# Attention on 64-query blocks: scores on quarters of the array, 13 transposes a pair of heads, and a split P V

## The chip, the cores and the metric

The kernel runs on one core of a Trainium2 chip. The metric is device time in microseconds (us) of one execution. The core has TensorE (PE; its weight loads are listed as PEld), VectorE (DVE), ScalarE (ACT), GpSimd (POOL) and SyncE (SP), whose queue issues all DMAs here.

## The reference

```
def _attn_ref(q, k, v):                     # 4 batches, 8 heads, 576 tokens, 64 channels
    scores = scale * np.matmul(q, k.transpose(0, 1, 3, 2))
    rel = pos[:, None] - pos[None, :]
    bias = slopes[:, None, None] * (-np.abs(rel))[None, :, :]
    mask = (rel >= 0) & (rel < 128)
    scores = np.where(mask, scores + bias[None], -1000000000.0)
    attn = np.exp(scores - max); attn = attn / (sum + 1e-09)
    return np.matmul(attn, v)
def _moe_ref(x, w1, w2, w3, w_out):   return ((x @ w1) * (x @ w2) @ w3) @ w_out     # 2304 x 512, ff 1024
def _moe2_ref(x, w_in, w_out):        h = np.maximum(x @ w_in, 0.0); return h * h @ w_out   # ff 2048
reference = _moe2_ref(_moe_ref(attention output laid out as 2304 x 512))
```

A query sees itself and the 127 keys before it. So 64 consecutive queries need at most 191 keys, and 128 consecutive queries at most 255.

## The kernel before, in words

The kernel is one program of small tasks. A planner (class `Plan`) is given each task's engine or engines, an assumed cost, the tasks that it depends on and the buffers that it holds; it lists the tasks in one order, and every engine executes its instructions in that order. A task with several possible engines (a copy, a normalisation, a conversion) gets the one that the planner picks. When costs, buffers or dependencies change, the whole order before the end of attention changes with them.

Attention works on pairs of heads: 32 heads are 16 pairs, head 2m on partitions 0 to 63 of the `qk` tile and head 2m+1 on 64 to 127. For each pair:
- `t_load_qk`, `t_load_v`: DMAs of q and k (transposed on the host) and of v into one of two fixed `v` tiles.
- `p_qk` (L451): the scores. A head is cut into four tiles of 128 queries with 128, 256, 256 and 256 keys and a last one with 192 keys, whose 64 queries stand on partitions 64 to 127. Each matmul has 64 rows (the channels) by 128 columns of the array, and the two heads alternate, so two matmuls lie on the two halves of the array. The task comes in three groups (`g` 0 to 2) into PSUM tiles `s`, of which there are four.
- `l_min` (L418, DVE): adds the bias tile `bm`, scales, and gives the row's minimum, into `e` (the last tile of a head into `p4`, named `p` in the profile). Five instructions a head.
- `l_exp` (L426, ACT): exponential with the row's sum. `l_sum` (L433, L434), then `l_norm` (L241 on DVE, L243 on ACT, L239 on POOL) divides by the sum. Five of each a head.
- `p_tr` (L467): 128 x 128 transposes of the probabilities on TensorE, nine a head in groups of four and five, into the one PSUM tile `t`; `l_pt` copies each group to `pt` (L199 on ACT).
- `p_pv` (L483): P V with v as the stationary operand, 128 rows by 64 columns of the array, the two heads on the two halves of the columns. Two groups a pair, six matmuls each, into the one PSUM tile `a`.
- `t_xh`, `t_xl`, `t_xs`: for batch 0 the result is split into a rounded part and a rest (`x`), for batches 1 to 3 it is copied to `xs` and stored to `x_scr`.

Between these tasks the planner sets those of the feed-forward part that can begin: conversions of packed weights (`raw`, L317, L326, L332, L202), w3 times w_out (`p_w34`, L589: 64 matmuls of 512 columns), and from 143 us on the first products of batch 0 (`p_ab`, L194 to L196, on `x` and `wu`). The last P V of the sixteenth pair ends at 210 us; from then on TensorE executes the rest of the two feed-forward nets.

At the start GpSimd makes the identity `ident` and the bias tile (`bm`, L220 to L228); four matmuls of `ident` and `bm` (`p_warm`, L515) stand ahead of the first scores in TensorE's order.

Of the kernel before, what the change touches and what calls it, by code (L numbers as in the profile page):

```python
# [15 lines left out]
RANK = dict(w34=4, h0=-20, w12=35.93, w12s=7.96, w12l=7.68, mg=500, mgs=4, yl=8, yn=0, hs=12)  # L16
# [7 lines left out]
NE = 3  # L24
# [7 lines left out]
class Plan:  # L32
# [27 lines left out]
    def run(self):  # L60
# [15 lines left out]
        shape = lambda n: {"qk": 1, "pv": 2}.get(n[:2], 0)  # L76
# [75 lines left out]
def fused_kernel(  # L152
# [48 lines left out]
    def sub(eng, o, a, b):  # L201
# [16 lines left out]
    bm = at.tile([128, H, 2 * WIN], F32, name="bm")  # L218
    b0 = bm[:, 0]
    nc.gpsimd.iota(  # L220
        b0, pattern=[[4, 2 * WIN]], base=-4 * WIN, channel_multiplier=-4,
        allow_small_or_imprecise_dtypes=True,
    )
    nc.gpsimd.affine_select(
        out=b0, in_=b0, pattern=[[-1, 2 * WIN]], compare_op=ALU.is_ge,
        fill=-1.0e30, base=WIN, channel_multiplier=1,
    )
    nc.gpsimd.affine_select(  # L228
        out=b0, in_=b0, pattern=[[1, 2 * WIN]], compare_op=ALU.is_gt,
        fill=-1.0e30, base=0, channel_multiplier=-1,  # L230
    )
    for h in range(1, H):
        nc.vector.tensor_scalar(out=bm[:, h], in0=b0, scalar1=0.5 ** h, scalar2=None, op0=ALU.mult)
# [38 lines left out]
    def w_dma(kb, n=1):  # L272
# [4 lines left out]
            u=11, u34=4, wo=4, qk=2, v=2, e=NE, p4=3, s=4, t=1, pt=NE, a=1, g=2, asb=2, gf=2, gt=8, ye=2,  # L277
            al=2, be=2, ga=2, d1=2, d2=2, d4=2, gq=8, xs=1, xm=1, xt1=1, xt2=1, yA=14, yB=6, s0=1, t2a=1, t2b=1, v6=6, st=2, xa=2, xb=2, xc=2, D1=2, D2=2, D4=2, D3=1, fo=4, fq=5, ww=4,
# [89 lines left out]
    QA = 384  # L368
    vt = [at.tile([128, 2, 5, D], F32, tag=f"v{i}", name=f"v{i}") for i in range(2)]
    for t in vt:  # L370
        nc.gpsimd.memset(t[64:128, :, 4, :], 0.0)
    p4 = [at.tile([128, 256], F32, tag=f"p4{i}", name=f"p4{i}") for i in range(3)]
    for t in p4:
        nc.gpsimd.memset(t, 0.0)
    stat = [at.tile([128, 3, 5], F32, tag=f"st{i}", name=f"st{i}") for i in range(4)]
    for t in stat:
        nc.gpsimd.memset(t, 1.0)
# [21 lines left out]
    def rows(i):  # L399
        return slice(64, 128) if i == 4 else slice(0, 128)  # L400

    def part_of(n, i):
        if i == 4:
            return p4[n % 3][64:128, 0:192]
        return HD[n]["e"][:, i, 128 if i == 0 else 0:256]

    def l_min(n, i):
        d = HD[n]
        bmh = bm[:, n % H]
        if i == 0:  # L410
# [12 lines left out]
    def l_exp(n, i):
        e = part_of(n, i)
        st = stat[n % 4][rows(i)]
        nc.scalar.activation(  # L426
            out=e, in_=e, func=ACTF.Exp, bias=st[:, 0, i:i + 1], scale=-1.0,
            accum_out=st[:, 1, i:i + 1],
        )

    def l_sum(n):
        st = stat[n % 4]
        nc.vector.tensor_scalar(out=st[:, 2], in0=st[:, 1], scalar1=1.0e-9, scalar2=None, op0=ALU.add)  # L433
        nc.vector.reciprocal(out=st[:, 2], in_=st[:, 2])  # L434

    def l_norm(n, i, e):
        x = part_of(n, i)
        scaled(e, x, x, stat[n % 4][rows(i), 2, i:i + 1])

    def p_qk(m, g):  # L440
# [962 lines left out]
```

## Time and profile before

| what | value |
|---|---|
| three runs | 845.72, 847.19, 847.26 us; median 847.19 |
| the profiled execution | 845.38 us, its span 843.4 us |
| granted TensorE clock | 0.999 |
| PE busy | 823.2 us (98%), 5830 matmul records |
| DVE busy | 629.7 us (75%) |
| ACT busy | 494.3 us (59%) |
| POOL busy | 61.1 us (7%) |
| DMA | 137.06 MB, mean 163 GB/s |

The span runs from the first to the last instruction; 1.98 us of the execution lie around it. TensorE's busy time is a union of records that overlap each other, so 98% does not say that no time is lost on it. An fp32 matmul leaves two records (two passes), a transpose or a matmul of the rounded type (`fp32r`) one.

### The profile page before, as it was taken

To read this page: it belongs to the slowest core of one execution; us is meant where nothing else is said; L and a number is where in the kernel's file an instruction comes from. 1 tells how busy PE (TensorE), PEld (TensorE's weight loads), DVE (VectorE), ACT (ScalarE), POOL (GpSimd) and SP (SyncE) were. 2 spreads that over 40 slices of the span, in tenths; PEclk is the share of its full clock that TensorE was granted. 3 is DMA by queue.
4 is the path that set the end of the run, shared out by engine and by line. 5 is a ranking of instruction groups with operands and counts; after the bars stand their busy time and mean duration, and the time that the engine had idled before them with its cause. 6 is when DMAs were issued, how large, how long until landed. Compare 5 with 4: busy or idle time off the path is not lost.

```text
span 843.4 us, 15493 instructions
## 1 busy us (share of the span) xinstructions
PE 823.2 (98%) x5830; PEld 752.8 (89%) x5830; DVE 629.7 (75%) x1354; ACT 494.3 (59%) x1026; POOL 61.1 (7%) x75
## 2 busy tenths in 40 slices
PE   7999999999999999999999999999999899999998
PEld 5555555879999989999999999999999799999998
DVE  7999897987689797497488574632599898767662
ACT  6997788986232361252225375744697776666531
POOL 1000010000000210030022031000112010000000
PEclk9999999999999999999999999999999999999999
DMA  9899789686423444112132364523796655444300
GB/s 277 263 305 312 247 262 271 189 286 239 126 75 121 143 154 145 49 39 65 61 107 97 132 188 150 184 102 108 235 294 205 186 157 150 138 140 133 98 33 32
DMA packets 92346, 137.06 MB, mean 163 GB/s; under 512 B 8304, under 2 KB 70256, under 8 KB 90224
## 3 DMA queue, kind: packets, MB, share of 16 engines
q1 hardware_dynamic: 92272, 136.08, 50.9%
q8 instruction: 46, 0.75, 0.4%
q14 instruction: 28, 0.23, 0.1%
HBM read 94.24 MB, written 41.81 MB: 161 GB/s over the span
## 4 chain that ended last, share of the span: by engine, by line
PE 76%; DVE 16%; ACT 4%; issue 2%; DMA 1%; POOL 0%; SPq 0%; ACTq 0%; DVEq 0%; POOLq 0%
PE xa L1061 8%; PE xa L1063 8%; PE xa L1062 8%; PE g L194 6%; PE g L195 6%; PE g L196 6%; PE xb L1061 4%; PE xb L1063 4%; PE xb L1062 4%; DVE e L418 3%; PE al L1010 3%; PE al L1012 2%; PE al L1011 2%; PE xc L1062 2%; PE xc L1061 2%
## 5 line engine op out<-in xcount | busy, mean ns | idle before, releaser
L1122 DVE TENSOR_TENSOR D<-xb,D 128x384 f32<-128x384 f32 (+1 forms) x66 | 34.0, 518 | 58.5 <-PE xb L1063 29.7
L195 PE MATMUL g<-gt,wu 128*128 128x288 f32 x256 | 75.7, 296 | 0.0
L194 PE MATMUL g<-gt,wu 128*128 128x288 f32 x256 | 75.7, 296 | 0.0
L196 PE MATMUL g<-gt,wu 128*128 128x288 f32 x256 | 75.4, 295 | 0.0
L426 ACT ACTIVATE e<-e,st 128x256 f32<-128x256 f32 (+1 forms) x128 | 60.5, 475 | 17.9 <-DVE st L418 17.5
L199 ACT ACTIVATE D<-xa 128x384 f32<-128x384 f32 (+1 forms) x102 | 46.3, 455 | 39.2 <-PE xa L1063 36.5
L589 PE MATMUL g<-raw 128*128 128x512 f32 x128 | 62.6, 604 | 0.3 <-DVE raw L332 0.3
L1010 PE MATMUL al<-x,wc 128*128 128x288 f32 x192 | 57.4, 299 | 2.0 <-ACT d L199 1.4
L202 DVE TENSOR_TENSOR ww<-fq,ww 128x1024 fp32r<-128x1024 f32 x34 | 41.6, 1223 | 23.1 <-ACT ww L199 22.7
L199 ACT ACTIVATE ww<-fq 128x1024 fp32r<-128x1024 f32 x35 | 37.0, 1058 | 34.7 <-PE xa L1063 19.7
L1012 PE MATMUL al<-x,wc 128*128 128x288 f32 x192 | 56.7, 295 | 0.0
L1011 PE MATMUL al<-x,wc 128*128 128x288 f32 x192 | 56.5, 294 | 0.0
L1152 ACT ACTIVATE D<-D 128x384 f32<-128x384 f32 x72 | 37.1, 523 | 25.5 <-DVE D L1122 25.4
L199 ACT ACTIVATE ye<-g 128x288 f32<-128x288 f32 x32 | 13.1, 410 | 66.0 <-PE g L196 61.9
L798 DVE TENSOR_TENSOR st<-st 128x256 f32<-128x256 f32 (+1 forms) x105 | 41.7, 428 | 11.1 <-DMA st<-m_scrc 6.1
L199 ACT ACTIVATE d<-al 128x288 f32<-128x288 f32 x72 | 29.2, 410 | 33.9 <-PE al L1012 26.1
L418 DVE CUSTOM_DVE_ANT_0 e<-s,bm 128x256 f32<-128x256 f32 (+1 forms) x128 | 43.3, 387 | 7.6 <-PE t L467 4.3
L195 PEld LDWEIGHTS g<-gt,wu 128*128 128x128 f32 x256 | 48.3, 189 | 0.0
L196 PEld LDWEIGHTS g<-gt,wu 128*128 128x128 f32 x256 | 48.2, 188 | 0.0
L194 PEld LDWEIGHTS g<-gt,wu 128*128 128x128 f32 x256 | 48.1, 188 | 0.1
L451 PE MATMUL s<-qk 64*128 64x256 f32 (+2 forms) x320 | 42.6, 369 | 2.5 <-DVE st L418 1.3
L483 PEld LDWEIGHTS a<-pt,v 128*64 128x64 f32 x384 | 23.6, 136 | 19.2 <-issue 5.9
(271 smaller groups left out, 2829.8 us busy)
## 6 DMA issues: line engine op xcount, KB each, us to landing
s_scr<-D SPq DMA_DIRECT2D x96, 192.0 KB, 2.0
u<-in_w2io_dram SPq DMA_DIRECT2D x22, 512.0 KB, 6.5
fo<-s_scr SPq DMA_DIRECT2D x20, 512.0 KB, 4.9
qk<-in_qk_dram SPq DMA_DIRECT2D x32, 288.0 KB, 5.6
st<-m_scrc SPq DMA_DIRECT2D x18, 512.0 KB, 3.7
raw<-in_w3t_dram SPq DMA_DIRECT2D x8, 1024.0 KB, 9.3
raw<-in_w_dram SPq DMA_DIRECT2D x8, 1024.0 KB, 6.9
fq<-s_scr SPq DMA_DIRECT2D x16, 512.0 KB, 5.0
```

The costliest lines, as they stand in the source:

```text
L194: nc.tensor.matmul(o, wh, xh, start=start, stop=False)
L195: nc.tensor.matmul(o, wh, xl, start=False, stop=False)
L196: nc.tensor.matmul(o, wl, xh, start=False, stop=stop)
L199: nc.scalar.activation(out=o, in_=i, func=ACTF.Copy)
L418: nc.vector.tensor_tensor_reduce(out=part_of(n, i), in0=ps, in1=bmi, op0=ALU.add, op1=ALU.min, scale=-0.125, scalar=3.0e38, accum_out=stat ...
L589: nc.tensor.matmul(gw[fi], wl, wr, start=c == 0, stop=c == 7)
L1010: nc.tensor.matmul(o, wh, xh, start=start and c == 0, stop=False, skip_group_check=True)
L1011: nc.tensor.matmul(o, wh, xl, start=False, stop=False, skip_group_check=True)
L1012: nc.tensor.matmul(o, wl, xh, start=False, stop=c == 1, skip_group_check=True)
L1061: nc.tensor.matmul(o, wh, xh, start=start, stop=False, skip_group_check=True)
L1062: nc.tensor.matmul(o, wh, xl, start=False, stop=False, skip_group_check=True)
L1063: nc.tensor.matmul(o, wl, xh, start=False, stop=stop, skip_group_check=True)
```

## The change

The same attention, cut otherwise. Each 64 queries get their own 192 keys; two such blocks stand above each other in a 128-row tile. A score tile is therefore 128 or 192 columns wide and never 256, and the bias comes in two new tiles, `bw` and `bz`, which GpSimd makes in five pieces (`toeplitz`). The score matmuls use 64 rows by 64 columns of the array; a tile takes four of 128 columns (the first one) or six of 192, 128 and 64. The last 64 queries of the two heads share one tile (`x` = 8), so a pair has nine exponentials and nine normalisations where it had ten of each; the minima stay ten. The probabilities of a pair stand in one tile `e` of 25 units of 64 columns; 13 transposes (in groups of 4, 4, 4 and 1) turn two units each, so that the two 64-row halves of a transposed tile can belong to different blocks of keys. P V is split: `p_pv` has 14 matmuls with 128 rows, 192 or 64 columns wide, and `p_pvl` has 14 with 64 rows by 64 columns of the array and 64 wide, which add into the same PSUM tiles; `t_load_v` loads parts of v a second time for them, to the other half of the partitions. The result leaves in pieces of 256, 64 and 256 columns instead of 384 and 192, and `xs` becomes a part of `pt`. Buffers: `e` and `pt` two of a pair each (before: three of a head), `s` three (four), `a` two (one). The first half of batch 0's products now waits for both pieces of `x`. Two weights of the planner (`w34`, `hs`) change.

```diff
-RANK = dict(w34=4, h0=-20, w12=35.93, w12s=7.96, w12l=7.68, mg=500, mgs=4, yl=8, yn=0, hs=12)
+RANK = dict(w34=3, h0=-20, w12=35.93, w12s=7.96, w12l=7.68, mg=500, mgs=4, yl=8, yn=0, hs=10)
-NE = 3
+NE = 2
+NPS = 3
...
-    ps_s = psb.enter_context(tc.tile_pool(name="ps_s", bufs=4, space=PSUM))
+    ps_s = psb.enter_context(tc.tile_pool(name="ps_s", bufs=NPS, space=PSUM))
     ps_t = psb.enter_context(tc.tile_pool(name="ps_t", bufs=1, space=PSUM))
-    ps_v = psb.enter_context(tc.tile_pool(name="ps_v", bufs=1, space=PSUM))
+    ps_v = psb.enter_context(tc.tile_pool(name="ps_v", bufs=5 - NPS, space=PSUM))
...
+    toeplitz(bz[:, 0], 0, True, False)
+    toeplitz(bw[0:64, 0, 64:256], 128, True, True)
+    toeplitz(bw[64:128, 0, 0:192], 128, True, True)
+    toeplitz(bw[64:128, 0, 192:256], 128, False, True)
+    toeplitz(bw[0:64, 0, 0:64], 0, True, False)
     for h in range(1, H):
-        nc.vector.tensor_scalar(out=bm[:, h], in0=b0, scalar1=0.5 ** h, scalar2=None, op0=ALU.mult)
+        nc.vector.tensor_scalar(out=bw[:, h], in0=bw[:, 0], scalar1=0.5 ** h, scalar2=None, op0=ALU.mult)
+        nc.scalar.activation(out=bz[:, h], in_=bz[:, 0], func=ACTF.Copy, scale=0.5 ** h)
...
-        nc.sync.dma_start(out=v[0:64, :, 4, :], in_=v_rest[b, 2 * p:2 * p + 2].rearrange("h p d -> p h d"))
+        nc.sync.dma_start(
+            out=v[64:128, :, 4:6, :].rearrange("p h c d -> p h (c d)"),
+            in_=v_main[b, 2 * p:2 * p + 2, 0:64, 2 * D:4 * D].rearrange("h p c -> p h c"),
+        )
+        nc.sync.dma_start(out=v[0:64, :, 4, :], in_=v_main[b, 2 * p:2 * p + 2, 64:128, 0:D].rearrange("h p d -> p h d"))
+        nc.sync.dma_start(out=v[0:64, :, 5, :], in_=v_rest[b, 2 * p:2 * p + 2].rearrange("h p d -> p h d"))
...
+        for i in ((0, 1, 2), (3, 4))[g]:
+            o = (0, 128, 320, 0, 192)[i]
+            if i == 0:
+                todo += [(r, x, 0, x, 0, 128) for x in range(2) for r in range(2)]
+            elif i == 4:
+                todo += [(r, r, o, 8, 6, 192) for r in range(2)]
+            else:
+                late = [i + 4 * r in LEFT_FIRST for r in range(2)]
+                todo += [(r, late[r], o, 2 * i + late[r], 2 * i - 2 + late[r], 192) for r in range(2)]
+                todo += [(r, 1 - late[r], o + 64 * late[r], 2 * i + 1 - late[r], 2 * i - 2 * late[r], 128) for r in range(2)]
+                todo += [(r, 1 - late[r], o + 128 - 128 * late[r], 2 * i + 1 - late[r], 2 * i - 1 + late[r], 64) for r in range(2)]
...
     PV = (
-        ((0, 0, 0, 256), (1, 128, 256, 256), (2, 256, 512, 128)),
-        ((3, 0, 768, 192), (2, 0, 640, 128), (4, 128, 960, 64)),
+        lambda r: ((0, 0, 512 * r, 192), (1, 192, 512 * r + 192, 64), (3, 256, 1152 + 192 * r, 64)),
+        lambda r: ((1, 0, 512 * r + 256, 64), (2, 64, 512 * r + 320, 64), (2, 128, 1024 + 192 * r, 64), (3, 192, 1088 + 192 * r, 64)),
     )
...
+    def p_pvl(m):
+        pt, v = PR[m]["pt"], vt[m % 2]
+        up, down = slice(0, 64), slice(64, 128)
+        todo = (
+            (0, up, 1, 128, lambda r: 512 * r + 384), (1, down, 5, 128, lambda r: 512 * r + 384),
+            (0, up, 4, 192, lambda r: 512 * r + 448), (1, down, 2, 192, lambda r: 512 * r + 448),
+            (1, down, 4, 0, lambda r: 1408 * r), (0, up, 5, 256, lambda r: 1408 + 64 * r),
+            (1, down, 1, 64, lambda r: 64 + 1408 * r),
+        )
...
-    XC = ((0, QA), (QA, S))
+    XC = (((0, 0, 256), (256, 512, 64)), ((0, 256, 256),))
...
-    W = (128, 256, 256, 256, 192)
+    W = (128, 192, 192, 192, 192)
...
-                [f"xl{g_}_{4 * b + k}" for g_ in range(hf + 1) for k in range(K1)] + [f"chw12{fi}", f"clw12{fi}", "gp"] + after
+                [f"xl{g_}_{4 * b + k}" for g_ in range(2) for k in range(K1)] + [f"chw12{fi}", f"clw12{fi}", "gp"] + after
```

How the instructions move is shown at three places; a row is an instruction with its line, what it writes and reads, the shape written, and how many alike follow each other. First TensorE in the early part, before: the first two groups of one pair's scores (L451), the transposes of a head (L467) and the first group of P V (L483), with w3 times w_out (L589) between them.

```order
L451 MATMUL s<-qk 128x128 x2
L451 MATMUL s<-qk 128x256 x6
L467 MATMUL t<-ident,e 128x128 x4
L589 MATMUL g<-raw 128x512 x2
L467 MATMUL t<-ident,p_139 128x128 x2
L467 MATMUL t<-ident,e 128x128 x3
L589 MATMUL g<-raw 128x512 x2
L483 MATMUL a<-pt,v_135 64x256 x4
L483 MATMUL a<-pt,v_135 64x128 x2
```

Now, on TensorE, the first group of a pair's scores (L467) and what stands behind it (L659 is w3 times w_out, L503 the transposes):

```order
L467 MATMUL s<-qk 64x128 x4
L467 MATMUL s<-qk 64x192 x2
L467 MATMUL s<-qk 64x128 x2
L467 MATMUL s<-qk 64x64 x2
L467 MATMUL s<-qk 64x192 x2
L467 MATMUL s<-qk 64x128 x2
L467 MATMUL s<-qk 64x64 x2
L659 MATMUL g<-raw 128x512
L503 MATMUL t<-ident,e 128x128 x4
```

Where two matmuls of 256 columns made one score tile of each head, six narrower ones on 64 columns of the array now do; the first group of scores holds 16 instructions in place of four. Second, on TensorE, P V of a pair now, with the last transpose ahead of it (L527 is `p_pv`, L543 is `p_pvl`):

```order
L503 MATMUL t<-ident,e 128x128
L527 MATMUL a<-pt,v_162 64x192 x2
L527 MATMUL a<-pt,v_162 64x64 x12
L543 MATMUL a<-pt,v_162 64x64 x8
L543 MATMUL a<-pl,v_162 64x64
L543 MATMUL a<-pt,v_162 64x64 x3
L543 MATMUL a<-pl,v_162 64x64
L543 MATMUL a<-pt,v_162 64x64
L659 MATMUL g<-raw 128x512 x3
```

The two groups of P V stand together and the quarter matmuls directly behind them, where before other work stood between the two groups. Third, GpSimd's first instructions, before:

```order
masks.py:197 MEMSET ident 128x128
L220 ISA
L220 IOTA bm 128x256
masks.py:199 AFFINE_SELECT ident<-ident 128x128
L224 AFFINE_SELECT bm<-bm 128x256
L371 MEMSET v_134 64x2x64
L228 AFFINE_SELECT bm<-bm 128x256
```

and now (`bz` and `bw` are the bias tiles):

```order
masks.py:197 MEMSET ident 128x128
L224 ISA
L224 IOTA bz 128x128
masks.py:199 AFFINE_SELECT ident<-ident 128x128
L229 AFFINE_SELECT bz<-bz 128x128
L224 IOTA bw 64x192 x2
L229 AFFINE_SELECT bw<-bw 64x192 x2
L234 AFFINE_SELECT bw<-bw 64x192 x2
L224 IOTA bw 64x64 x2
L234 AFFINE_SELECT bw<-bw 64x64
L229 AFFINE_SELECT bw<-bw 64x64
```

The last instruction on which the first matmul of TensorE waits (it reads `bw`) is the fourteenth there, counted without the row `ISA`, where it was the sixth.

## Rows read from the trace of the kernel before

**Rows 1.** Busy time by stretch: stretch, length, PE, PEld, DVE, ACT, POOL, clock, DMA share, GB/s.

```profile
8.00:66.00 58.00, 53.91 (x333) 33.11 (x331) 55.21 (x194) 54.97 (x148) 0.60 (x1) 1.00 0.92 299
66.00:104.00 38.00, 37.85 (x201) 20.59 (x203) 34.10 (x97) 27.59 (x71) 0.43 (x1) 1.00 0.84 278
104.00:172.00 68.00, 66.36 (x474) 45.45 (x471) 60.38 (x221) 60.75 (x181) 3.05 (x7) 1.00 0.82 238
172.00:212.00 40.00, 39.66 (x333) 33.70 (x332) 32.27 (x115) 30.34 (x84) 0.83 (x2) 1.00 0.79 270
212.00:843.00 631.00, 620.15 (x4475) 616.17 (x4474) 444.96 (x722) 319.14 (x544) 52.67 (x46) 1.00 0.40 128
```

**Rows 2.** The chain of waits by line, in 8 to 66, 104 to 172, 172 to 212 us.

```profile
by line: DVE e L418 20.3%; DVE raw L332 16.3%; DVE e L241 13.8%; DVE raw L326 7.7%; DVE p L418 6.1%; ACT raw L317 5.2%; DVE x L202 4.6%; issue 4.4%; DVE p L241 3.3%; DVE st L434 3.1%; ACT pt L199 2.7%; ACT p L426 1.9%; DVE st L433 1.9%; ACT
...
by line: DVE e L418 15.6%; DVE e L241 9.6%; DVE wu L202 7.9%; ACT e L426 7.4%; issue 5.5%; DVE raw L332 5.4%; DVE u L332 5.2%; ACT pt L199 3.9%; DVE p L418 3.8%; DVE p L241 3.3%; DVE raw L326 3.0%; DVE st L434 2.9%; ACT p L426 2.4%; PE s L4
...
by line: PE a L483 20.6%; PE t L467 19.3%; PE g L194 16.4%; PE g L195 14.9%; PE g L196 14.6%; PE s L451 11.9%; DVE u L332 3.1%; DVE e L418 1.6%; ACT pt L199 0.4%; issue 0.4%; DVE st L418 0.1%; ACTq L199 0.1%
```

**Rows 3.** TensorE's records on tile `a` (P V) by stretch: length, busy, records.

```profile
8.00:66.00 58.00, 8.72 (x96) 1.00 0.92 299
66.00:104.00 38.00, 4.70 (x52) 1.00 0.84 278
104.00:172.00 68.00, 12.75 (x144) 1.00 0.82 238
172.00:212.00 40.00, 8.72 (x96) 1.00 0.79 270
```

**Rows 4.** Pieces of the chain, 84 to 196 us: start, us until the next piece, records.

```profile
84.20 1.72 PE g L589 x4
...
87.15 1.72 PE s L451 x16
...
179.95 0.53 PE s L451 x4
180.47 0.81 PE a L483 x12
181.28 0.59 PE t L467 x4
...
195.55 1.23 PE a L483 x12
```

**Rows 5.** Groups by line and shape, 0 to 212 us: count, busy us, mean ns.

```profile
L426 ACT ACTIVATE e<-e,st 128x256 f32<-128x256 f32 x96 | 47.8, 500 | 1.0 <-DVE st L418 0.9
L199 ACT ACTIVATE pt<-t 128x512 f32<-128x512 f32 x64 | 37.7, 589 | 4.2 <-PE t L467 2.9 <-PE a L483 0.6
L418 DVE CUSTOM_DVE_ANT_0 e<-s,bm 128x256 f32<-128x256 f32 x96 | 36.5, 420 | 0.2
...
L241 DVE TENSOR_SCALAR e<-e,st 128x256 f32<-128x256 f32 x78 | 23.8, 356 | 0.0
...
L426 ACT ACTIVATE p<-p,st 64x192 f32<-64x192 f32 x32 | 14.4, 450 | 2.3 <-DVE st L418 1.7
...
L418 DVE CUSTOM_DVE_ANT_0 p<-s,bm 64x192 f32<-64x192 f32 x32 | 11.4, 361 | 1.3 <-PE s L451 0.3
...
L241 DVE TENSOR_SCALAR p<-p,st 64x192 f32<-64x192 f32 x23 | 7.4, 320 | 0.5
```

**Rows 6.** The chain at the start, same columns as rows 4.

```profile
0.73 0.12 POOL ident masks.py:197
...
2.25 0.41 POOL bm L228
2.70 3.70 PE t L515 x8
```

**Rows 7.** TensorE's timeline: two P V matmuls, 64 wide, alone: start, us, shape, records.

```profile
188.83 0.28 PE L483 MATMUL a<-pt,v 128*64 128x64 f32 x4
```

**Rows 8.** DMA of 0 to 215 us.

```profile
DMA packets 21237, 56.33 MB, mean 262 GB/s; under 512 B 4112, under 2 KB 8288, under 8 KB 19168
```

More of the change, by code (lines that the diff above doesn't have):

```diff
@@ L365, in add_weights @@
         add("cl" + k, rank, w_tt(1024), lambda e: conv_lo(key, e), ["ch" + k], [], ["raw" + k])
[L368 to L377, printed above, removed]
+    vt = [at.tile([128, 2, 6, D], F32, tag=f"v{i}", name=f"v{i}") for i in range(2)]
+    stat = [at.tile([128, 3, 9], F32, tag=f"st{i}", name=f"st{i}") for i in range(2)]
     HD = [dict() for _ in range(B * H)]
@@ L426, in l_exp @@
         nc.scalar.activation(
-            out=e, in_=e, func=ACTF.Exp, bias=st[:, 0, i:i + 1], scale=-1.0,
-            accum_out=st[:, 1, i:i + 1],
+            out=e, in_=e, func=ACTF.Exp, bias=st[:, 0, x:x + 1], scale=-1.0,
+            accum_out=st[:, 1, x:x + 1],
         )
     def l_sum(n):
[L432 to L438, printed above, removed]
+        m, r = divmod(n, 2)
@@ new lines, in p_qk, with p_tr @@
+        for a in todo:
+            mm(*a)
+    def p_tr(m, g):
+        e = PR[m]["e"]
+        t = PR[m]["t", g] = ps_t.tile([128, 512], F32, tag="t", name="t")
+        if g < 2:
+            todo = [(t[:, 128 * i:128 * i + 128], u) for i, u in enumerate(((0, 2, 8, 4), (11, 13, 23, 15))[g])]
+        elif g == 2:
+            todo = [
+                (t[:, 0:128], 6), (t[:, 128:512].rearrange("p (a c) -> p a c", c=192)[:, :, 0:64], 19),
+                (t[:, 192:320], 17), (t[:, 384:512], 21),
+            ]
+        else:
+            todo = [(t[:, 0:128], 9)]
+        for o, u in todo:
+            nc.tensor.transpose(o, e[:, u:u + 2, :].rearrange("p u c -> p (u c)"), ident)
@@ L480, in p_pv @@
         o = PR[m][g] = ps_v.tile([128, 512], F32, tag="a", name="a")
-        for x, (kb, c, src, w) in enumerate(PV[g]):
+        pt = PR[m]["pt"]
+        for x in range(len(PV[g](0))):
+            for r in range(2):
+                kb, c, src, w = PV[g](r)[x]
+                nc.tensor.matmul(
+                    o[64 * r:64 * r + 64, c:c + w], vt[m % 2][:, r, kb, :], pt[:, src:src + w],
+                    start=x == 0, stop=False, skip_group_check=True,
+                )
+    def p_pvl(m):
[6 more added lines that the diff above has]
+            (1, down, 1, 64, lambda r: 64 + 1408 * r),
+        )
+        for x, (g, rows, kb, c, src) in enumerate(todo):
@@ L514, in p_warm @@
         for _ in range(k):
-            nc.tensor.matmul(t[:, 0:w], ident, bm[:, 0, 0:w], start=True, stop=True)
+            nc.tensor.matmul(t[:, 0:w], ident, bw[:, 0, 0:w], start=True, stop=True)
     plan.filler = p_warm
@@ new lines, in add_pair @@
+                    [f"qk{i // 3}_{m}"] + ([f"mi{i - 1}_{n}"] if i else []) + ([f"mi0_{n - 1}"] if j and not i else []),
+                    [f"e_{m}"] if i == 0 and j == 0 else [], [f"s{i // 3}_{n}"],
+                )
+                if i < 4:
+                    add(f"ex{4 * j + i}_{m}", rj + 2.1, {"a": 0.29 + W[i] * 0.00086}, lambda e, i=i, j=j: l_exp(m, 4 * j + i), [f"mi{i}_{n}"])
+        add(f"ex8_{m}", r + 4.1, {"a": 0.29 + 192 * 0.00086}, lambda e: l_exp(m, 8), [f"mi4_{n}" for n in heads])
@@ L575, in add_pair @@
+        if b < NS:
+            hold(xn, f"x_{p}", 4 * NF1)
+        for g in range(2):
+            cost = {}
+            for _, _, w in XC[g]:
+                for k, v in w_copy(w, True).items():
+                    cost[k] = cost.get(k, 0) + v
+            add(f"xh{g}_{m}", r + 9, cost, lambda e, g=g: t_xh(m, g, e),
+                [f"pvl_{m}"] + ([f"xh0_{m}"] if g else []), [xn] if b < NS and not g else [], [f"{'ab'[g]}{m}"])
             if b < NS:
-                add(f"xl{g}_{m}", r + 9, w_tt(w, "d"), lambda e, g=g: t_xl(m, g), [f"xh{g}_{m}"], [], [f"{'ab'[g]}{m}"])
+                add(f"xl{g}_{m}", r + 9, {"d": sum(w_tt(w, "d")["d"] for _, _, w in XC[g])}, lambda e, g=g: t_xl(m, g),
+                    [f"xh{g}_{m}"], [], [f"{'ab'[g]}{m}"])
@@ L577, in add_pair @@
         if b >= NS:
[L578 removed]
+            add(f"sx{m}", r + 9, {"dma": w_dma(295)}, lambda e: t_xs(m), [f"xh{g}_{m}" for g in range(2)], [], [f"pt_{m}"])
     gw = {}
```

212 lines of the change are left out of this document (105 added, 107 removed).

## Prediction
> **What bounds the kernel now.** I read the stretches first. From 212 us to the end TensorE is busy 620.15 of 631 us, while VectorE and ScalarE are far from full [rows 1]. The change touches nothing there, so whatever moves the end moves the end of the attention part, and what it gives is what TensorE gets to do sooner before 212 us. Before that, three engines are near their limit at once, and the chain of waits says which one ends last. From 8 to 66 us it is mostly VectorE: the minima (L418), the normalisations (L241) and the conversions of weights (L332, L326), and VectorE is busy 55.21 of 58 us [rows 1, 2]. From 66 to 104 us TensorE is busy 37.85 of 38 us [rows 1]. From 104 to 172 us the chain is again mostly VectorE, with pieces of ScalarE (L426, L199); from 172 us it is TensorE: P V 20.6%, transposes 19.3%, scores 11.9%, products of batch 0 most of the rest [rows 2].
>
> A pair leaves 24 records on tile `a`, so by [rows 3] 96/24 = 4.0 pairs lie in 8 to 66, 52/24 = 2.2 in 66 to 104, 144/24 = 6.0 in 104 to 172 and 4.0 in 172 to 212. I price the change per pair: by TensorE in the 6.2 pairs of the second and fourth stretch, by VectorE and ScalarE in the 10.0 of the others.
>
> **TensorE, a pair before.** Two matmuls of 512 columns on the whole array took 1.72 us: 1.68 ns a column [rows 4]. The 16 records of scores are eight matmuls of together 2 x 128 + 6 x 256 = 1792 columns, which one after the other would be 3.01 us; the piece is 1.72 us long [rows 4]. So the two halves of the array work at the same time: 896 columns are 1.51 us, and 0.21 us is the group's own overhead. The last group, 192 columns deep, gives 0.32 + 0.21 = 0.53, the P V group of 0.81 us 384 columns deep and 0.16 over, and that of 1.23 us 640 deep and 0.16 over [rows 4]. Four transposes behind another kind of matmul are 0.59 us; a fifth adds 128 columns of one pass, 0.11. A pair is 1.72 + 0.53 + 1.23 + 0.81 + 2 x (0.59 + 0.70) = 6.87 us.
>
> **TensorE, a pair after.** The depth of the scores is 128 + 4 x 192 = 896 columns if the four quarters of the array work at once: 1.51 us, plus 0.21 for each of two groups, 1.93. P V on full rows is 320 + 256 = 576 deep, in one block by the order rows: 0.97 + 0.16 = 1.13. The 14 quarter matmuls are four rounds of 64 columns: 0.43 + 0.16 = 0.59. The transposes are 3 x 0.59 and a single one of 0.11 + 0.16: 2.04. Sum 5.69, or 1.18 us less a pair.
>
> No row shows four quarters at work. The nearest rows are halves by rows and halves by columns, both two at a time [rows 4]. If quarters too ran only two at a time, the scores' 24 matmuls of 3200 columns would be 1600 deep, 2.69 + 0.42 = 3.11 us, and the quarter P V 448 deep, 0.75 + 0.16 = 0.91: a pair 7.19 us, 0.32 more than before. I take four at a time, because neither the split by rows nor that by columns costs anything beyond the columns in these rows. The Trainium skill, TensorEngine Tiling (Array Packing), Key Properties, says that different tiles can load weights and multiply in parallel, and lists four independent tiles of 64 x 64; the trace agrees for two, and no run here shows four.
>
> **VectorE and ScalarE, a pair.** Six of the ten minima go from 256 to 192 columns: 0.420 to 0.361 us by mean duration, 0.35 us together; by busy time (36.5/96 = 0.380 against 11.4/32 = 0.356) only 0.14 [rows 5]. Of the normalisations VectorE has 78/16 = 4.9 wide ones a pair, 0.356 to 0.320, 0.18 us (nothing by busy time), and of two last tiles one goes, 23/32 of it on VectorE: 0.23. That is 0.37 to 0.76 us a pair; the result's third piece takes a few hundredths back in four pairs. On ScalarE six exponentials go from 0.500 to 0.450 and one of 0.450 goes: 0.75. The copies out of the transposes were 4 x 0.589 and become 3 x 0.589 and one of 128 columns, which I put at 0.3 (it is under the 0.450 of 192 columns): 0.29 less. One more copy of the result a pair costs about 0.3. Together 0.74. I take 0.65 us a pair, near VectorE's upper end because most of these instructions stand in rows behind each other's waits: 10.0 x 0.65 = 6.5 us.
>
> **The start.** TensorE's first matmul waits for the bias tile: GpSimd gets from 0.73 to 2.66 us with six instructions, 0.32 each; the matmuls behind it (3.70 us) and the scores follow at once [rows 6]. Now it is the fourteenth instruction. Eight more are 2.6 us at that rate, 1.0 at the shortest piece (0.12), 3.3 at the longest (0.41); the new pieces are narrower, so I take 2.2, all of it on the path, since every engine waits for the first scores.
>
> **What costs nothing, and its cover.** v is loaded with 96 KB more a pair, 1.5 MB in all, beside 56.33 MB at 262 GB/s [rows 8]: 5.9 us of transfers, spread over 16 pairs and issued two pairs ahead. The cover is thinnest in 8 to 66 us, where the engines of the DMA are busy 0.92 of the time [rows 1]; with no cover, four pairs there cost 1.5 us. Three score tiles instead of four make the second group of scores wait for three minima of the first; behind it on TensorE stand transposes and w3 times w_out, and up to 3 x 0.361 = 1.1 us a pair would be lost. Before, six tiles a pair went through four buffers, now four through three, so I count nothing. The products of batch 0 wait for one piece of `x` more, but the four pairs that make `x` are over at 66 us [rows 3] and the products begin at 143 us. Bringing `xs` into `pt` holds that buffer until its store has landed; two pairs lie between.
>
> **The sum.** 6.2 x 1.18 = 7.3, plus 6.5, minus 2.2: 11.6 us. From the profiled execution (845.4, that is its span of 843.4 and 2.0 around it) this gives 833.8, from the median of 847.2 it gives 835.6. I forecast 835 us.
>
> **The rivals.**
> - *TensorE is the bound throughout* (0.20). In 104 to 172 us it is busy 66.36 of 68 us and in 8 to 66 us 53.91 of 58 [rows 1]; if its order, not VectorE, holds the others up, all 16.2 pairs give 1.18: 19.1 - 2.2 = 16.9 us, 830, and down to 823. Against it: the chain names VectorE there.
> - *The stretches of VectorE give nothing* (0.12), because a wait for a score tile or for a pair's buffer takes the place of the shorter instructions: 7.3 - 2.2 = 5.1 us, 842.
> - *Nothing measurable* (0.04), about 847.
> - *Quarters work two at a time* (0.10), the case on the other side. TensorE loses 0.32 in 6.2 pairs, 2.0 us; in the other ten its 3.2 us more fill what it had free, and the shorter instructions of VectorE wait for it. With the start 4.2 us, 851, at most 855. It decides from the point where a pair's work on TensorE is not shorter than 6.87 us.
> - *Narrow matmuls cost a fixed time* (0.04). A pair now has 52 matmuls, 104 records, instead of 44. Two 64-wide ones alone took 0.28 us for four records [rows 7]; put wholly down to the records it is 0.07 each, and 60 more, two at a time, are 2.1 us a pair, 0.9 net: 16 x 0.9 + 2.2 = 17 us, 864. Against it: 64 columns, two at a time, are 0.11 of the 0.28, and 0.16 over is what any group shows. The Trainium skill, TensorEngine Tiling (Array Packing), Instruction Overhead, speaks for this rival: about 60 cycles a matmul, and no tiling factor from a dimension that is already small. By it the 30 more matmuls, 60 passes of 25 ns, would be an estimated 1.5 us a pair if nothing overlapped.
>
> **How the numbers follow.** Forecast 0.50 (830 to 841), the others as given. A measurement of this kernel tells about 0.2%, 1.7 us, from no change. Faster than that: 0.50 + 0.20 + 0.12 = 0.82; same 0.04; slower 0.10 + 0.04 = 0.14. The range of 824 to 848 holds the forecast, nearly all of the first rival, the second and the third: 0.84. The forecast alone, with the bounds of VectorE (0.37 to 0.76) and of the start (1.0 to 3.3), is 830 to 841.
>
> **What would show it.** Right: the granted clock at 1.00; a pair's 24 score matmuls in about 1.9 us where they are not held up; the last P V near 200 us with the same pieces of feed-forward ahead of it, or later with more of them; minima of 192 columns near 0.36 us; the first scores at about 8.6 us. Wrong: quarter matmuls that start in twos with their full depth between; a gap on TensorE ahead of the second score group that a minimum ends; transfers of v that end a wait; or a span after the last P V that is longer than before.

## The result and the profile after

The changed kernel takes 839.17 us (median of five runs, 835.16 to 839.85), the kernel before 847.19 us in the same runs (845.63 to 848.39). The ratio is 0.990, with a 95% interval of 0.9873 to 0.9927: 8 us faster, where 12 were forecast. The profiled execution of the change took 835.16 us (span 833.4), 10.2 us less than that of before.

The time is one that the forecast allowed; the way to it is not. The stretches of [rows 1], now in the changed kernel, in the same columns:

```profile
8.00:66.00 58.00, 54.23 (x608) 34.47 (x608) 51.05 (x194) 45.94 (x138) 2.90 (x4) 1.00 0.96 298
66.00:104.00 38.00, 38.00 (x427) 22.25 (x426) 31.06 (x115) 27.85 (x86) 0.82 (x2) 1.00 0.90 276
104.00:172.00 68.00, 67.42 (x905) 53.40 (x904) 63.35 (x248) 56.55 (x184) 3.57 (x4) 1.00 0.90 270
172.00:212.00 40.00, 31.54 (x373) 28.67 (x372) 20.08 (x68) 18.57 (x56) 0.00 (x0) 0.91 0.61 188
212.00:833.00 621.00, 610.50 (x4404) 606.72 (x4402) 443.10 (x721) 317.61 (x541) 52.22 (x46) 1.00 0.43 135
```

Up to 172 us TensorE is as full as before or fuller, and it gets more done: the first products of batch 0 begin at 125.6 us (143 before). But from 172 to 212 us it is busy only 31.54 of 40 us (39.66 before). VectorE and ScalarE are idle half of that time as well, so none of the three bounds the stretch.

The chain of waits of the changed kernel from 172 us on (start, us until the next piece, what) names what does:

```profile
172.72 0.33 SPq L843
...
173.10 5.92 DMA u<-in_w2io_dram
...
179.13 1.10 ACT u L330
180.23 0.99 ACT u L335
181.22 0.16 ACT pl L200
...
194.23 7.10 DMA m_scri<-u
...
201.43 0.70 DVE wc L260
```

These are not the attention's transfers. Eight tiles of packed w2 weights are loaded (`m_load`, L843), converted on ScalarE and VectorE (L330, L335, L339, L345) and stored again (`m_store`, L849), to be fetched after 400 us. I call this a round trip. The planner sets the conversions into the same queues as the attention's copies, and there they wait for their loads: at 179.13 ScalarE has just got its load, and only behind the conversion comes the copy `pl` (L200) for which P V waits. The waits for a DMA of 120 to 212 us (who waited for what: us in total, times, longest), first the four that matter in the changed kernel, then all of those before:

```profile
ACT u L330 <- DMA u<-in_w2io_dram: 13.7, 5, 5.0
DVE wc L260 <- DMA m_scri<-u: 11.0, 2, 8.1
DVE u L339 <- DMA u<-in_w2io_dram: 3.9, 2, 2.6
DVE u L345 <- DMA m_scri<-u: 2.3, 1, 2.3
```

```profile
DVE u L326 <- DMA u<-in_w2io_dram: 1.3, 1, 1.3
DVE st L798 <- DMA st<-m_scrc: 0.9, 1, 0.9
ACT u L317 <- DMA u<-in_w2io_dram: 0.2, 1, 0.2
PEld a L483 <- DMA m_scri<-u: 0.2, 1, 0.2
```

The same eight round trips were there before, but when VectorE and ScalarE came to a conversion, its load had nearly always landed: 1.5 us of waits for these loads, now 17.6. One link lies behind this. The tiles `u` and the weights of batch 1, `wc`, take their buffers from the same eleven slots, and the slot of a stored tile comes free only when its store has landed. The loads in SyncE's queue (L843; L773 before) waited for that four times in 120 to 212 us, before only once, and `wc` waited for it on VectorE, 11.0 us in the list. First the changed kernel, then the one before:

```profile
SPq L843 <- DMA m_scri<-u: 21.3, 4, 6.2
```

```profile
SPq L773 <- DMA m_scri<-u: 4.3, 1, 4.3
```

So these loads started late, and the engines reached their conversions early; no run separates what each of the two made of the 17.6 us. (The changed kernel has one longer wait for a DMA, of GpSimd for v, 16.4 us; GpSimd has little to do there, 3.57 of 68 us.)

A pair's work on TensorE, in pieces of the chain from 108 us (to be read against [rows 4]):

```profile
108.41 0.81 PE s L467 x12
...
109.48 1.17 PE a L527 x28
110.66 0.62 PE a L543 x28
...
116.65 1.04 PE s L467 x25
```

The two groups of scores take 1.04 and 0.81 us, 1.85 together (1.93 forecast), P V 1.17 and 0.62 (1.13 and 0.59). Four quarters do work at once: two at a time, the scores would take 3.11 us. The shorter instructions of VectorE and ScalarE, by line and shape (against [rows 5]), are as expected too:

```profile
L443 ACT ACTIVATE e<-e,st 128x192 f32<-128x192 f32 x112 | 50.1, 450 | 2.4 <-DVE st L435 2.1
...
L435 DVE CUSTOM_DVE_ANT_0 e<-s,bw 128x192 f32<-128x192 f32 x96 | 31.6, 351 | 4.5 <-PE s L467 4.5
L467 PE MATMUL s<-qk 64*64 64x192 f32 x256 | 30.8, 330 | 0.5 <-DVE st L435 0.5
```

And the start is 2.3 us later (against [rows 6]; the scores came at 6.40 there):

```profile
4.66 0.24 POOL bw L229
...
4.95 3.78 PE t L569 x8
8.73 1.29 PE s L467 x17
```

### The profile page after: what moved, and what is told of

Same layout as the page of the kernel before. It is cut to its first block, busy times and chain, and to the rows that moved or that the text cites. A ratio compares the mean times of both kernels' runs of the same rounds, so it can differ in the third digit from the quotient of the medians.

```text
span 833.4 us, 17233 instructions
## 1 busy us (share of the span) xinstructions
PE 804.7 (97%) x6716; PEld 748.0 (90%) x6716; DVE 610.1 (73%) x1349; ACT 469.3 (56%) x1011; POOL 63.3 (8%) x74
## 4 chain that ended last, share of the span: by engine, by line
PE 80%; DMA 8%; DVE 6%; ACT 3%; issue 1%; SPq 1%; POOL 0%; POOLq 0%; ACTq 0%; DVEq 0%
PE xa L1131 8%; PE xa L1133 8%; PE xa L1132 8%; PE g L659 6%; PE g L195 5%; PE g L196 5%; PE g L197 5%; PE xb L1133 4%; PE xb L1131 4%; PE xb L1132 4%; DMA m_scri<-u 3%; PE al L1080 3%; PE al L1082 3%; PE al L1081 3%; PE s L467 2%; DMA u<-in_w2io_dram 2%
## 5 line engine op out<-in xcount | busy, mean ns | idle before, releaser
L195 PE MATMUL g<-gt,wu 128*128 128x288 f32 x256 | 76.7, 300 | 0.0
L196 PE MATMUL g<-gt,wu 128*128 128x288 f32 x256 | 76.3, 298 | 0.0
L197 PE MATMUL g<-gt,wu 128*128 128x288 f32 x256 | 76.1, 297 | 0.0
L443 ACT ACTIVATE e<-e,st 128x128 f32<-128x128 f32 (+1 forms) x144 | 62.5, 438 | 13.7 <-DVE st L435 13.1
L200 ACT ACTIVATE D<-xa 128x384 f32<-128x384 f32 (+1 forms) x102 | 46.2, 454 | 38.5 <-PE xa L1133 35.2
L659 PE MATMUL g<-raw 128*128 128x512 f32 x128 | 61.0, 603 | 0.0
L200 ACT ACTIVATE ww<-fq 128x1024 fp32r<-128x1024 f32 x35 | 37.0, 1058 | 34.9 <-PE xa L1133 19.3
L200 ACT ACTIVATE ye<-g 128x288 f32<-128x288 f32 x32 | 13.1, 411 | 69.8 <-PE g L197 62.3
L196 PEld LDWEIGHTS g<-gt,wu 128*128 128x128 f32 x256 | 48.9, 191 | 0.0
L197 PEld LDWEIGHTS g<-gt,wu 128*128 128x128 f32 x256 | 48.8, 191 | 0.0
L195 PEld LDWEIGHTS g<-gt,wu 128*128 128x128 f32 x256 | 48.6, 190 | 0.1
L503 PEld LDWEIGHTS t<-ident,e 128*128 128x128 f32 x208 | 24.4, 142 | 26.0 <-ACT pt L200 15.9
L200 ACT ACTIVATE d<-al 128x288 f32<-128x288 f32 x71 | 28.8, 409 | 31.4 <-PE al L1082 25.2
L503 PE MATMUL t<-ident,e 128*128 128x128 f32 x208 | 36.0, 286 | 8.9 <-ACT pt L200 8.8
L435 DVE CUSTOM_DVE_ANT_0 e<-s,bw 128x192 f32<-128x192 f32 (+1 forms) x128 | 40.9, 351 | 4.8 <-PE s L467 4.5
```

The source lines that it names most:

```text
L195: nc.tensor.matmul(o, wh, xh, start=start, stop=False)
L196: nc.tensor.matmul(o, wh, xl, start=False, stop=False)
L197: nc.tensor.matmul(o, wl, xh, start=False, stop=stop)
L200: nc.scalar.activation(out=o, in_=i, func=ACTF.Copy)
L443: nc.scalar.activation(out=e, in_=e, func=ACTF.Exp, bias=st[:, 0, x:x + 1], scale=-1.0, accum_out=st[:, 1, x:x + 1],)
L659: nc.tensor.matmul(gw[fi], wl, wr, start=c == 0, stop=c == 7)
```

## The experiments

Three theories stood against each other for 160 to 212 us. **A**: the round trips hold up ScalarE and VectorE, and through them TensorE. **B**: the second loads of v hold up the queue of the DMAs. **C**: nothing is lost; the stretch only has more work of batch 0 in it. Besides these, the terms of the forecast's sum were to be taken apart. As a measure of where the attention part leaves the kernel I take the start of the first product of batch 1 (tile `al`) on TensorE: all attention and the first net of batch 0 lie ahead of it. It is read from one profile of each run; in the two profiles of the changed kernel it lies 3.9 us apart (239.8 and 243.7).

**The change again**, beside the first three experiments.

> The changed kernel once more, beside the experiments on the same chip: 0.987 to 0.993 of the kernel before. Theory A (the round trips of the packed w2 weights hold up ScalarE, VectorE and with them TensorE from 160 to 212 us) expects the same stretch with TensorE busy about 43 of 52 us again, and the granted clock of the whole run between 0.989 and 0.995, the longer runs with the lower clock.

Measured: 838.87 us, ratio 0.9905 (0.9887 to 0.9924). TensorE busy 44.11 of 52 us in 160 to 212: the gap is there again.

**Round trips behind the attention.** Their first load depends on the last pair's P V.

```diff
-    prev = [f"clw12{i}" for i in range(8)]
+    prev = [f"clw12{i}" for i in range(8)] + [f"pvl_{B * H // 2 - 1}"]
```

> The changed kernel with one dependency more: the loads of the w2 weights that are converted and stored again wait, in the planner, for the quarter P V of the sixteenth pair. Theory A: the last P V comes near 195 us in place of 208.5, TensorE is busy all the time there, and the end is 8 to 11 us earlier than the changed kernel's, ratio to the kernel before about 0.979. Theory B (the second loads of v hold up the queue of SP and the DMA engines): those loads stay, so the stretch stays long, gain under 2 us. Theory C (the stretch is long because 21 tasks of batch 0 instead of 16 lie in it, nothing is lost): no gain, or a loss, since the conversions now lie beside TensorE's later work, 0.990 or more.

Measured: 849.70 us, ratio 1.0036 (1.0024 to 1.0047). By stretch:

```profile
160.00:212.00 52.00, 51.82 (x631) 49.19 (x630) 25.66 (x107) 30.77 (x101) 1.13 (x3) 1.00 0.51 157
212.00:260.00 48.00, 42.58 (x297) 41.54 (x295) 36.76 (x64) 17.36 (x29) 0.00 (x0) 0.93 0.84 281
260.00:460.00 200.00, 186.74 (x1354) 183.96 (x1355) 159.97 (x320) 67.72 (x135) 30.20 (x21) 0.97 0.28 92
```

The gap closes and `al` begins at 227.4 us instead of 239.8, as A says and C does not. But the whole gain and more is lost up to 460 us. From 205 to 300 us TensorE now waits for weights of batch 1, whose making shares VectorE and the slots of tile `u` with the conversions (the wait of the weight load; that of the matmul itself is listed apart with 8.2 us):

```profile
PEld al L1080 <- DVE wc L260: 8.6, 2, 4.5
```

So where the round trips lie was shown to matter; that they can be had for nothing was not.

**Second loads of v left out.** The quarter matmuls read blocks of v that are there anyway, so the values of P V are not the reference's; two loads a pair are gone.

```diff
-        nc.sync.dma_start(
-            out=v[64:128, :, 4:6, :].rearrange("p h c d -> p h (c d)"),
-            in_=v_main[b, 2 * p:2 * p + 2, 0:64, 2 * D:4 * D].rearrange("h p c -> p h c"),
-        )
-        nc.sync.dma_start(out=v[0:64, :, 4, :], in_=v_main[b, 2 * p:2 * p + 2, 64:128, 0:D].rearrange("h p d -> p h d"))
...
-                    PR[m][g][64 * r:64 * r + 64, c:c + 64], v[rows, r, kb, :], (PR[m]["pl"] if g and x >= 4 and not r else pt)[rows, src(r):src(r) + 64],
+                    PR[m][g][64 * r:64 * r + 64, c:c + 64], v[rows, r, kb if rows == up and kb == 5 else kb % 4, :], (PR[m]["pl"] if g and x >= 4 and not r else pt)[rows, src(r):src(r) + 64],
```

> The changed kernel without the two further loads of v a pair (96 KB a pair, 32 DMAs in all); the quarter matmuls read parts of v that are there, so their values are others, with the same matmuls. Theory A: the waits for the w2 weights stay, gain 0 to 2 us, ratio 0.988 to 0.991. Theory B: the stretch from 160 to 212 us closes up, gain 6 to 10 us, ratio about 0.980.

Measured: 837.63 us, ratio 0.9892 (0.987 to 0.9915), an interval that holds the 0.9905 of the change; TensorE is busy 45.99 of 52 us in 160 to 212. B falls.

**A shorter start.** The matmuls ahead of the first scores (L569) read only `ident` and no longer wait for `bw`.

```diff
-        for _ in range(k):
-            nc.tensor.matmul(t[:, 0:w], ident, bw[:, 0, 0:w], start=True, stop=True)
+        for _ in range(k * w // 128):
+            nc.tensor.matmul(t[:, 0:128], ident, ident, start=True, stop=True)
```

> The changed kernel with the first matmuls of TensorE working on the identity alone (the same columns in pieces of 128), so that they need not wait for the bias tile. If the start costs what the profile says (the first scores at 8.73 in place of 6.40 us) and the delay is carried to the end, 2 us earlier, ratio about 0.988. If the round trips of theory A take up whatever comes earlier, the scores start near 6 us and the end does not move by more than 1 us.

Measured: 840.05 us, ratio 0.9918 (0.9903 to 0.9934): no gain. The first scores come at 5.23 us, 3.5 us sooner, but the time is lost again before 56 us. Its first 24 us, and behind them the same three stretches of the changed kernel:

```profile
0.00:8.00 8.00, 6.32 (x53) 5.63 (x54) 1.98 (x10) 2.92 (x9) 3.82 (x18) 1.00 0.75 170
8.00:16.00 8.00, 6.23 (x83) 4.55 (x83) 7.43 (x48) 7.33 (x31) 0.00 (x0) 1.00 1.07 288
16.00:24.00 8.00, 6.44 (x100) 5.23 (x101) 4.97 (x26) 4.17 (x13) 0.00 (x0) 0.57 0.69 258
```

```profile
0.00:8.00 8.00, 3.05 (x7) 2.52 (x8) 1.50 (x7) 2.79 (x8) 3.82 (x18) 1.00 0.74 168
8.00:16.00 8.00, 7.41 (x108) 5.70 (x110) 5.16 (x34) 5.18 (x24) 0.00 (x0) 1.00 1.00 279
16.00:24.00 8.00, 6.94 (x136) 5.27 (x127) 7.79 (x43) 7.48 (x27) 0.00 (x0) 1.00 0.79 278
```

The granted clock of 16 to 24 us is 0.57, close to its lower level of 1.2 GHz (0.50), where the changed kernel had 1.00; TensorE had been busy 6.32 and 6.23 us in the two stretches ahead, in the changed kernel 3.05 and 7.41. An estimate from these rows: 8 us at 0.57 are 3.4 us short of 8 us at full clock, about what had been won. So this is no clean test of the start: what it shows is that 3.5 us won there did not reach the end, not what 3.5 us would be worth at the full clock.

**No early round trips.** The eight tiles are loaded and converted when their use comes near.

```diff
-    m_scr = {(k, m): dram.tile([128, 1024], F32, name=f"m_scr{k}{m}") for k in "ic" for m in range(NM)}
+    m_scr = {(k, m): dram.tile([128, 1024], F32, name=f"m_scr{k}{m}") for k in "c" for m in range(NM)}
```

> The changed kernel without the early round trips of the eight tiles of w2 that are needed last: they are loaded and converted only when their use comes near (around 420 to 500 us), so between 138 and 240 us there are no such loads, conversions and stores at all. Theory A (the round trips hold TensorE up between 160 and 212): TensorE over 51 of 52 us busy there, last P V near 195 us, and 826 to 833 us if the late conversions lie beside other work; if they don't, the gain is seen until 400 us and is lost between 420 and 500 us. Theory C (the stretch is long only because of the work ahead in it): TensorE's busy share in 160 to 212 stays near 44 of 52 and the total near 839.

Measured: 827.23 us (826.54 to 827.89), ratio to before 0.9768 (0.975 to 0.9785), 12 us faster than the change. Two stretches of it:

```profile
160.00:212.00 52.00, 51.83 (x631) 49.19 (x629) 25.57 (x108) 29.77 (x98) 1.11 (x3) 1.00 0.35 108
460.00:560.00 100.00, 98.03 (x549) 96.23 (x548) 61.61 (x101) 64.97 (x127) 13.77 (x14) 1.00 0.54 180
```

TensorE is full, and `al` begins 12.6 us sooner than in the changed kernel (16.5 than in its second profile, 243.7). Of the 12.6, 5.0 are given back later: the last product `xa` of the kernel begins at 819.6 us against 827.2, only 7.6 sooner. From 460 to 560 us, where the late conversions lie, TensorE is busy 98.03 us instead of 100.00, and VectorE 61.61 instead of 53.57.

The gap was not only waiting. Everything from 8 us to the first `al`, first in the changed kernel, then without round trips:

```profile
8.00:239.80 231.80, 218.44 (x2511) 165.81 (x2511) 185.92 (x660) 158.09 (x479) 7.29 (x10) 0.99 0.83 256
8.00:227.20 219.20, 214.38 (x2511) 163.33 (x2510) 173.54 (x641) 153.76 (x478) 10.78 (x14) 1.00 0.70 216
```

TensorE was idle 13.36 us against 4.82, and busy 4.06 us longer with as many records (2511). So of the 12.6 us, 8.5 were waits and 4.1 the same work taking longer; the granted clock of 200 to 210 us was 0.66 in the changed kernel and 1.00 without round trips.

**The same edit in the kernel before**, as a control: is the gain one of the edit alone?

> The kernel before with the same edit as in the run without the early round trips: the eight tiles of w2 that are needed last are loaded and converted only near their use. In the kernel before TensorE was busy 51.66 of 52 us in 160 to 212, so there is little to win there. If the round trips cost only where the change had emptied TensorE's queue (theory A): 843 to 849, at most 0.5% under the kernel before. If they cost the same in any kernel, and the gain of the edit is one of its own: 834 to 837, 12 us less as in the changed kernel.

Measured: 853.46 us, ratio 1.0091 (1.0073 to 1.0109). There the edit costs 7.6 us. TensorE had no gap to close, and the late conversions take their price. Of the 7.6, 1.6 lie ahead of `al`; the granted clock of 155 to 160 us was 0.66 here (1.00 in the kernel before), and TensorE was busy 1.2 us longer up to `al` with as many records. The first product `al` in four kernels (count: shortest, median, longest ns, first and last start), in the order before, changed, before without round trips, changed without them:

```profile
L1010 PE MATMUL al<-x,wc x192: 290/296/402, 248.4 to 448.8; 128*128 128x288 f32 x192
```

```profile
L1080 PE MATMUL al<-x,wc x192: 288/296/402, 239.8 to 439.4; 128*128 128x288 f32 x192
```

```profile
L1010 PE MATMUL al<-x,wc x192: 288/296/402, 250.0 to 451.2; 128*128 128x288 f32 x192
```

```profile
L1080 PE MATMUL al<-x,wc x192: 288/296/403, 227.2 to 426.6; 128*128 128x288 f32 x192
```

With the round trips in place the change brings `al` 8.6 us forward, without them 22.8 (the medians of the whole time lie 26.2 us apart). So the change itself is worth some 22.8 us in the attention part, 21.2 if `al` without round trips is set against the kernel before as it stands. Of the 14.2 us between 22.8 and 8.6, 12.6 are what the round trips cost the changed kernel (16.5 by its second profile), in waits and in clock, and 1.6 what the edit costs the kernel before.

**Round trips later still**: they begin when the weights of batch 1 are made (`prev = [f"wlbc{FO[OB][-1]}{OB}"]` in the line of the first experiment), in the changed kernel and in the one before.

> The changed kernel with the round trips of the packed w2 tiles neither beside the attention nor left out, but later: the first of them may start when the last weights of batch 1 are made. Between 260 and 460 us ScalarE is busy 78 of 200 us and the transfers take a third of the DMA engines' time. The attention part as in the run without the round trips: first records of the products al near 227 us. If what that run lost again after 460 us came from its late conversions (5.7 us of its 13), this one loses 0 to 2 us of it: 821 to 825. If the round trips take slots from the weights of batches 2 and 3, it loses between 280 and 440 us what it wins: 827 to 835.

> The same edit in the kernel before. There TensorE had no gap between 160 and 212 us to be closed: 845 to 849, about as the kernel before, if the round trips find room after 260 us. The distance from this run to the one with the same edit in the changed kernel is what the change is worth with the round trips out of its way: 22 to 26 us if the reading holds that TensorE sets the pace of the attention in both kernels, 11 us if the prediction's sum was right and the late stretch took nothing.

Measured: 840.54 us (ratio 0.9913, 0.989 to 0.9936) and 870.49 us (1.0272, 1.0248 to 1.0297). `al` begins at 226.2 us against 249.6, 23.4 sooner, but lasts until 441.4 and 470.7: products that took 200 us take 215 and 221. The two kernels lie 30 us apart, more than the 22 to 26 expected, as the one before also loses more after 260 us. The room that I saw there by ScalarE's and the transfers' shares is not to be had: TensorE waits for weights of the batches again (one wait of 6.5 us for `wc` in the changed kernel).

**Three early round trips.** Only tiles 3 to 5 keep theirs (`... for k in "ic" for m in range(NM) if k == "c" or 3 <= m < 6`).

> The changed kernel with three of the eight early round trips kept (those of the tiles 3 to 5), the other five tiles loaded and converted late as in the run without any. In the changed kernel the first three round trips lay before 180 us, where TensorE was still busy 18.84 of 20 us in 160 to 180; the five behind them lay where it was busy 17.23 of 25 us. If the cost in the attention part comes from the later ones, this run keeps TensorE at 50 to 51 of 52 us in 160 to 212 and loses less after 485 us than the run without any: 823 to 828. If each round trip costs the same, three of eight cost about 5 us of the 13 in the attention part: 829 to 833.

Measured: 828.27 us, ratio 0.9781 (0.9761 to 0.9802), not to be told from no round trips, and just above the 823 to 828 that I expected. `al` begins at 228.6 us: by these profiles the first three cost about 1.4 us, so the other five cost the rest of the 12.6. What it loses there it wins back from 460 to 560 us, where TensorE is full again:

```profile
160.00:212.00 52.00, 49.91 (x605) 46.25 (x603) 29.25 (x104) 27.15 (x90) 2.18 (x2) 1.00 0.46 144
460.00:560.00 100.00, 100.00 (x568) 99.82 (x567) 56.42 (x96) 64.14 (x128) 13.46 (x13) 1.00 0.49 167
```

**Two figures of the planner.** It adds 3.0 us to a load's transfer time until the first use; a slot counts as free 0.1 us after its store. First only the 3.0 are set to 6.0, then also the 0.1 to 4.5.

```diff
-        dict(pe=0.25, a=0.3, d=0.22, p=0.25, dma=3.0, gate=0.0),
+        dict(pe=0.25, a=0.3, d=0.22, p=0.25, dma=6.0, gate=0.0),
...
-                    pool[self.holds[h][0]].append(last[h] + 0.1)
+                    pool[self.holds[h][0]].append(last[h] + (4.5 if e == "dma" else 0.1))
```

> Half of the edit of the run before: only the 6.0 us from a load's issue to its first use, the slots come free as before. If the wait of ScalarE for the loads is the larger part (13.1 us against 11.0 of VectorE for slots), this alone brings 3 to 5 us (834 to 836); if the wait for the slot of a store is, it stays at 838 to 840 and only the run with both improves.

> The changed kernel with the planner told what the trace shows of transfers: 6.0 us instead of 3.0 from a load's issue to the first use, and a slot that a store gives back counts as free 4.5 us after it instead of 0.1. The work and its sizes are the same, only the order changes. Theory A: the conversions stand later in the queues of ScalarE and VectorE, so they no longer stop for a load in front of copies that TensorE needs: TensorE 47 to 51 of 52 us busy in 160 to 212, total 831 to 837. Theory C: 839 as before.

Measured: 883.04 us (ratio 1.0416, 1.0395 to 1.0436) and 889.55 us (1.0502, 1.0481 to 1.0523). In 160 to 212 us both are as A says, 52.00 of 52 us busy. But the weights of the later batches come too late. The first with its figure of 6.0 alone: a stretch, and the group of products with its busy time, mean ns, and idle time before them:

```profile
260.00:460.00 200.00, 170.03 (x1141) 164.67 (x1142) 136.63 (x266) 53.12 (x106) 13.19 (x8) 0.90 0.22 72
```

```profile
L1080 PE MATMUL al<-x,wc 128*128 128x288 f32 x192 | 62.5, 325 | 31.4 <-DVE wc L260 25.7
```

In the changed kernel that group had 1.3 us of idle time. My expectation misread the first figure: the planner adds it to the transfer time that it reckons itself, 3.5 us for such a load (1048 KB at its 300 KB a us), so it already counted 6.5, and a load's median is 6.1 us in the trace. I made a fair figure too long, for every load of the program. The figure that is wrong is the store's: 1.75 us (524 KB) and 0.1, where the stores of the changed kernel took 2.8 to 7.1. That one alone was not tried.

**The widths alone.** In the kernel before, minima, exponentials and normalisations of the middle tiles on 192 columns; `e` becomes three fixed, zeroed tiles, and 64 keys are left out of these rows' softmax.

```diff
-    W = (128, 256, 256, 256, 192)
+    W = (128, 192, 192, 192, 192)
...
-            c0 = 128 if i == 0 else 0
-            o = (i % 2) * 256
+            c0 = 128 if i == 0 else 64
+            o = (i % 2) * 256 + c0 * (i > 0)
```

> The kernel before with one part of the change alone: minima, exponentials and normalisations of the two middle tiles of a pair on 192 of their 256 columns; the other 64 columns of the exponentials stay at zero, so it leaves 64 keys out of the softmax of these tiles and its values are not the reference's. Matmuls, transposes and loads are those of before. By the prediction's sum the widths gain only where VectorE and ScalarE bound, 0.65 us a pair in about 6 pairs: 843 us. If they were the greater part of the whole change: 838 to 840. If a wait takes their place: 847, no change.

Measured: 845.40 us against 847.31, ratio 0.9979 (0.996 to 0.9998): 1.9 us, by the interval 0.2 to 3.4. The expectation took 0.65 us in six pairs, 3.9. The prediction's sum has ten pairs; for the widths alone its bounds on VectorE are 0.14 us a pair by busy time and 0.53 by duration, 1.4 and 5.3 us.

## Why the prediction came out near, and what was wrong in it

**TensorE a pair: a little too small, and counted in too few pairs.** 1.18 us were forecast. TensorE's busy time by line from 0 to 230 us, without round trips: scores, transposes and P V, first in the kernel before (L451, L467, L483), then in the changed one (L467, L503, both kinds of P V on tile `a`):

```profile
0.00:230.00 230.00, 41.82 (x320) 0.99 0.64 200
0.00:230.00 230.00, 44.67 (x288) 0.99 0.64 200
0.00:230.00 230.00, 35.58 (x384) 0.99 0.64 200
```

```profile
0.00:230.00 230.00, 34.99 (x768) 1.00 0.70 212
0.00:230.00 230.00, 35.53 (x208) 1.00 0.70 212
0.00:230.00 230.00, 29.90 (x896) 1.00 0.70 212
```

That is 122.07 against 100.42 us, 21.65 less, or 1.35 in each of 16 pairs (time in which two of these lines overlap is counted twice). The step that failed is the split of the pairs: I priced 6.2 by TensorE and 10.0 by VectorE and ScalarE. By `al` 22.8 us came out, so all pairs gave what TensorE saved. TensorE's idle time up to `al` hardly changed, 9.35 and 9.77 us: it waited 2.3 us longer for its first matmul and 1.8 less after 8 us. The some 1.6 us of busy time that are left include the slower clock of the control; I cannot assign the rest. The first rival, TensorE as the bound throughout (16.9 us with the start taken off), had the mechanism of the attention part. What spoke against it, that the chain names VectorE in 104 to 172 us, was a poor reason: TensorE was busy 66.36 of 68 us there, and a chain that runs through VectorE beside a TensorE so full says little of what a shorter matmul is worth.

**VectorE and ScalarE, 6.5 us: too large as a term of its own.** The widths alone, in the kernel before, give 1.9 us, near the lower of the two bounds (1.4). The prediction took 0.65 us a pair, near VectorE's upper end.

**The start, 2.2 us: its size right (2.3), its place on the path not shown.** The earlier start did not reach the end, though at a lower clock on the way; that run also kept the round trips, which could have taken up what came earlier.

**"What costs nothing": right for v, and one thing missing.** Leaving out the second loads changes nothing that can be measured, and three score tiles held up nobody (TensorE waited 0.5 us for minima ahead of all its 192-wide score matmuls). The list held only transfers of the attention. The round trips beside it were hidden while VectorE and ScalarE had full queues and the loads came early, and I shortened these queues without asking what else stands in them. In the changed kernel that cost 12.6 us ahead of `al`, more than any term of the sum, and it has the form of the second rival (a wait takes the place of the shorter instructions) with another cause than the ones named there.

**The sum.** 11.6 us were forecast from three terms. What happened in the attention part is 22.8 less 14.2, 8.6 by `al` (4.7 by the second profile). Two errors of opposite sign left the number near: that the forecast came out near is luck.

**Rivals that fell.** Quarters two at a time: scores in 1.85 us. A fixed time for narrow matmuls: the 28 records of quarter P V take 0.62 us, forecast 0.59 from columns alone. The Trainium skill, TensorEngine Tiling (Array Packing), Instruction Overhead, spoke for that rival with about 60 cycles a matmul; no such sum on top of the columns is seen here. A span after the attention that is longer than before: from the first `al` to the last the changed kernel takes as long as the one before.

## What to carry to other kernels

Before shortening an engine's work, list what else stands in its queue and what that waits for: here loads of some 6 us cost next to nothing behind full queues and became stalls in front of the critical copies when the queues emptied. If an edit gives less than its parts, take the neighbour that now stalls out of both kernels and compare again; the control in the kernel before is what tells a loss of the change from a gain of the edit. And price a shorter matmul in every stretch where TensorE is nearly full, whichever engine the chain of waits names there.

## What the runs showed of the hardware

In the changed kernel the clock fell around the stretch in which TensorE waited: in the profiled run it was busy 17.23 of 25 us from 180 to 205, and the granted clock of 200 to 210 us was 0.66; in the other profile of the same kernel the fall lay ahead of 205 us (0.93 for 180 to 205, 1.00 for 200 to 210). Not every wait was followed by a fall: TensorE was busy 3.05 of the first 8 us, and up to 24 us the clock stayed at 1.00. The five runs of the change, spread over 4.7 us, had mean clocks of 0.989 to 0.995; without the round trips, at 0.998 in its profile, the runs lie within 1.4 us.
